# A Fourier filter and gated convolution on one core: the first input in longer rows over all DMA engines, the weights behind it, and the order laid out anew

## The chip, the cores and the metric

The kernel runs on one core of one Trainium2 chip. The metric is device time in microseconds (us) of one execution, the median of several runs. A profile is one further execution with the hardware profiler on; its times are counted from the first instruction.

## What is computed

Eight batches, each of 3200 positions by 256 channels, all float32 (three of the later weights come as float64). First a filter in frequency space:

```
X  = rfft(x, axis=1)
Yr = Xr @ w_r - Xi @ w_i + b_r
Yi = Xr @ w_i + Xi @ w_r + b_i
Y  = soft threshold of Yr and Yi at 0.01
y  = irfft(Y, n=3200)
```

Then a gated causal convolution of five taps on y:

```
gate = sigmoid(sum over k of conv_w[k] * y shifted by 4 - k)
out  = (gate * (y @ w_val)) @ w_out
```

## The kernel before

The transform of length 3200 is split as 64 x 50. For each batch the work goes through these steps, named by the tiles that appear in a profile:

- `x` is loaded in 8 blocks `u`, each of two halves `h`. A half is 50 rows of 4 KB; half 0 stands on partitions 0 to 49, half 1 on 64 to 113. TensorE (PE) multiplies it with `f1` (tile `f_sb`) into `p`, a copy keeps that as `s`, and a DMA stores it to `a_dram` in HBM. The store turns the two axes of the split.
- `a` is read back in 13 units of 128 rows. PE makes `s` (tile `s2`, printed `s`) from `a` and the matrix `f2`, then ScalarE (ACT) and VectorE (DVE) split it into a high and a low part (`xs`, `sx`), and PE does the complex product with the weights in `k_ps` (the sum of real and imaginary part) and `y_ps`. The weights `w_sb` are split likewise: `load_matrix` loads `w_r` and `w_i` into `st`, ACT casts the high part, DVE subtracts for the low part, and `sums` makes the sum and the difference of both.
- Bias and threshold follow (`yb`, `tp`), then `z_ps` (the first half of the way back), stored to `z_dram`, read back as `zl`, and `y_p`, which lands in `y_sb`. `turned` makes the way back's matrix `g1` from `f2` by PE with an identity, `eye`.
- The convolution runs on DVE (`acc`), `v_ps` and `o_ps` are the two products of the second layer.

What sets the order is `Plan`: every piece of work is entered by `add` with an engine, an estimated length, a place `at`, what it uses and what it sets. `Plan.order` plays the pieces through in time and takes on each engine, among those that could begin within `SLACK` of the first, the one with the smallest `at`. The table `O` shifts the `at` of each kind of work, `CLOCK`, `WIRE` and `BACKLOG` are its assumptions on PE and on transfers. What comes out is a fixed order of instructions on each engine; on the chip each engine follows its own, waiting for semaphores. Transfers are issued by SyncE (SP) and, at the start, by ACT. The compiled program gives the transfers eight semaphores in turn, so that an issue waits until the transfer eight places before it has landed.

The start of the program is written apart, in `p1_first`, for batch 0. It takes the eight blocks in four groups `v` of two. SP loads the halves `h = 0` and ACT the halves `h = 1`; each group gives 8 products on PE (16 instructions in a profile), a copy on DVE for one half and on ACT for the other, and four stores, two on SP and two on ACT. Two PSUM tiles of the kind `ps_2` hold a group's products, so the next group begins when both copies are done. Between the groups stand products `warm`, which compute nothing; `WARM` says how many. `STORED` stands for all stores of batch 0, and `load_f2` loads the matrix `f2` in four parts, the parts behind the first only after `STORED`. `load_bias` loads the two biases onto one partition, and PE spreads them over all partitions by six matmuls (lines 449 and 451). `from_float64` converts float64 weights to float32 in 13 steps on DVE, at `at + O["later"]`.

Of the kernel before, what the change touches and what calls it, by code (L numbers as in the profile page):

```python
# [32 lines left out]
def dft_constants():  # L33
# [46 lines left out]
class Plan:  # L80
# [30 lines left out]
    def order(self):  # L111
# [101 lines left out]
WEIGHTS = 130  # L213
CLOCK = ((40000, 1.6), (45000, 1.15))
WIRE = 230
BACKLOG = 5000


# [4 lines left out]
def act(n, kind="copy"):  # L223
# [5 lines left out]
T = float(NU)  # L229
O = {'hold': -1.089,  # L230
     'together': 2.272,
     'later': 4.406,
     'load_x': -3.369,
     'p1': 1.752,
     'p1_step': 1.14,
     'load_a': -3.927,
     's2': -1.558,
     's1i': 1.333,
     'p3': 3.595,
     'load_z': -3.135,  # L240
     'y': 0.522,
     'conv': 1.176,
     'val': 2.74,
     'gate': -3.751,
     'project': 5.91,
     'late_val': 7.079,
     'late_out': 15.503,
     'turn': 0.967,
     'mix_sum': -0.635,
     'p1_1': -0.586,  # L250
     'load_x_1': -0.349,
     'p1_2': -1.603,
     'p3_0': 0.549}
WARM = 2, 1, 1, 1, 10
SLOTS = {"x": 3, "zl": 3, "y_hl": 2, "s1": 2, "a": 3, "xs": 2, "sx": 2, "xz": 1, "yb": 2, "tp": 3, "zst": 2,
         "acc": 2, "g_hl": 2, "o": 2, "ps_s2": 2, "ps_y": 1, "ps_k": 1, "ps_2": 2, "a_dram": 2, "z_dram": 2}
# [6 lines left out]
def fourier_filter_then_gated_conv(ctx: ExitStack, tc: tile.TileContext, x, w_r, w_i, b_r, b_i,  # L263
# [57 lines left out]
    def load_matrix(at, name, w, dst):  # L321
# [87 lines left out]
    def load_f2(at, part):  # L409
        t = slice(PARTS[part] * 2 * P, min(PARTS[part + 1] * 2, NT) * P)  # L410
        add(at, "SP", 400, lambda: nc.sync.dma_start(out=f2_sb[:, t], in_=f2[:, t]), STORED if part else (), [("f2", part, 0)],
            kb=(t.stop - t.start) / 2)

# [14 lines left out]
    def load_bias(at):  # L428

        def load():  # L430
            for k, b in enumerate((b_r, b_i)):
                nc.sync.dma_start(out=b_sb[0:1, k * D:(k + 1) * D], in_=b.rearrange("(o d) -> o d", o=1))
        add(-91, "SP", 800, load, (), [("b", 0, 0)], kb=20)

        def marks():
# [3 lines left out]
            nc.gpsimd.memset(m[:, P + N1 + 1:], 1.0)  # L439
        add(-198, "POOL", 300, marks, (), [("b", 0, 1)])  # L440
        k2, k1 = ("bias_2", 0), ("bias_1", 0)
        m = lambda k: b_sb[0:1, 2 * D + k * P:2 * D + (k + 1) * P]

        def spread():
# [5 lines left out]
            for k in range(2):  # L450
                nc.tensor.matmul(q, m(k), b_sb[0:1, k * D:(k + 1) * D], start=k == 0, stop=k == 1)
        add(at, "PE", 2700, spread, [("b", 0, 0), ("b", 0, 1)], [k2 + (0,), k1 + (0,)], {k2: "ps_y", k1: "ps_k"}, mode="f")
        add(at + 0.01, "ACT", act(2 * D), lambda: nc.scalar.copy(out=bias_sb[:, 0:2], in_=tl[k2]), [k2 + (0,)], [("bias", 0, 0)])
# [30 lines left out]
    STORED = [("stored", 0, (u, h)) for u in range(8) for h in range(NH)]  # L484

    def p1_first(v, at):

        us = (2 * v, 2 * v + 1)
        src = x[0].rearrange("(n h m) c -> h n (m c)", h=NH, m=NM)
        engines = (("SP", nc.sync), ("ACT", nc.scalar))  # L490
        for u in us:
            kx, tag = ("x", (0, u)), "x" if u < 3 else "zl" if u < 6 else "y_hl"

            def load(h, u=u, kx=kx, tag=tag):
                xt = tl[kx] if h else room(kx, tag, 4 * D)
                engines[h][1].dma_start(out=xt[half(h), :], in_=src[h, :, u * 4 * D:(u + 1) * 4 * D])
            for h in range(NH):
                add(-100 + u, engines[h][0], 400, lambda h=h, load=load: load(h), (), [kx + (h,)], None if h else {kx: tag}, kb=200)
        kp = [("p1", (0, v, h)) for h in range(NH)]
# [3 lines left out]
        def products():  # L503
            p = [two_banks(kp[h]) for h in range(NH)]
            for j in range(2):
                for h in range(NH):
                    for k in range(2):
                        nc.tensor.matmul(p[h][k * HP:(k + 1) * HP, j, :], f1_sb[half(h), :],
                                         tl["x", (0, us[k])][half(h), j * 512:(j + 1) * 512], start=True, stop=True)

# [4 lines left out]
        def store(h, k):  # L515
            if ("a_dram", 0) not in tl:
                buffer(("a_dram", 0), "a_dram", [Q, NM * D])
            dst = tl["a_dram", 0].rearrange("(f h) mc -> h f mc", h=NH)
            engines[h][1].dma_start(out=dst[h, :, us[k] * 4 * D:(us[k] + 1) * 4 * D], in_=tl[ks[h]][k * HP:k * HP + N2, :])
        add(at, "PE", 1740, products, [("x", (0, u), h) for u in us for h in range(NH)] + [("f1", 0, 0)],  # L520
            [k + (0,) for k in kp] + [("turn", "p1", v)], {k: "ps_2" for k in kp}, mode="q")
        for h, eng in enumerate(("DVE", "ACT")):
            add(at + 0.01, eng, act(1024) if h else dve(1024), lambda h=h: keep(h), [kp[h] + (0,)],
                [ks[h] + (0,)] + ([START[h]] if v == 3 else []), {ks[h]: tag})
            for k in range(2):
                add(at + 0.02, engines[h][0], 400, lambda h=h, k=k: store(h, k), [ks[h] + (0,)], [("a_dram", 0, (us[k], h)), ("stored", 0, (us[k], h))],
                    {("a_dram", 0): "a_dram"} if (v, h, k) == (0, 0, 0) else None, kb=200)

    def p1(b, u, at):

        kx, kp, ks, ka = ("x", (b, u)), ("p1", (b, u)), ("s1", (b, u)), ("a_dram", b)
# [18 lines left out]
        def store():  # L550
# [4 lines left out]
            for k in range(2):  # L555
                lo = u * 4 * D + k * 512
                nc.sync.dma_start(out=dst[:, :, lo:lo + 512], in_=st[k * HP:k * HP + N2])
        add(at + O["load_x"] + O["load_x_1"] * (b == 1), "SP", 700, load, STORED if b == 1 else (), [kx + (0,)], {kx: "x"}, kb=400, chain="x")
        add(at, "PE", 890, products, [kx + (0,), ("f1", 0, 0)], [kp + (0,)], {kp: "ps_2"}, mode="q")
        add(at + 0.01, "ACT", act(1024), keep, [kp + (0,)], [ks + (0,)], {ks: "s1"})  # L560
        add(at + 0.02, "SP", 1500, store, [ks + (0,)], [ka + (u,)], {ka: "a_dram"} if u == 0 else None, kb=400)


# [421 lines left out]
```

## Time and profile before

| what | value |
| --- | --- |
| median of 3 runs | 900.66 us (899.45 to 905.88) |
| profiled execution, first to last instruction | 897.1 us |
| mean TensorE clock granted | 0.986 |
| PE busy | 865.2 us (96%) |
| weight loads (PEld) | 741.1 us (83%) |
| DVE busy | 763.5 us (85%) |
| ACT busy | 603.7 us (67%) |
| moved by DMA | 162.26 MB, mean 181 GB/s |

The profiled execution has no other time of its own than this span; the timed runs, which hold what lies around it too, take 3.6 us more in the median. In a profile, L508 is line 508 of the kernel; names of tiles stand as out<-in. PE is the matmul engine, PEld its weight loads, which run beside it; SPq and ACTq are the issues of transfers by SP and ACT. A matmul in float32 is counted as two instructions, so that `x8` can be four matmuls of the program. The share of DMA is the mean of the core's 16 DMA engines.

### The profile page before, as it was taken

Reading aid. Unit: us, or ns where it says so; the run is one execution under the profiler, and the core shown is the slowest. Engines: PE = TensorE matmul, PEld = TensorE weight load, DVE = VectorE, ACT = ScalarE, POOL = GpSimd, SP = SyncE. Lnnn points to the kernel's source line nnn. Section 1 sums busy time; section 2 is a strip of 40 time slices with the busy share of each in tenths; the row PEclk is TensorE's granted clock in tenths of the full one; section 3 lists DMA queues with packets and bytes.
Section 4 is the critical chain, followed back from the end, with each engine's and each line's share of the span. In section 5 each row is a group of like instructions: output and inputs, shape, how many; then the busy total and the mean of one; then the engine's idle time right before and its main releaser. Section 6 shows DMA issues by size and latency. Waiting matters only on the chain.

```text
span 897.1 us, 24381 instructions
## 1 busy us (share of the span) xinstructions
PE 865.2 (96%) x10370; PEld 741.1 (83%) x10370; DVE 763.5 (85%) x1139; ACT 603.7 (67%) x924; POOL 4.4 (0%) x11
## 2 busy tenths in 40 slices
PE   7799979999999999999999999999999999999898
PEld 2478758898888988899888988989788899998675
DVE  1267787999899997999789996999969998999896
ACT  1256656877677867777677876877757776875654
POOL 0000000000000000000000000000001000000000
PEclk8889999999999999999999999999999999999999
DMA  6577777635755476555674566645674453513522
GB/s 203 198 233 239 228 227 217 210 130 182 236 180 179 159 229 218 190 183 160 217 235 158 163 204 217 222 131 174 215 223 154 139 172 109 178 62 116 180 75 91
DMA packets 103439, 162.26 MB, mean 181 GB/s; under 512 B 9154, under 2 KB 77636, under 8 KB 103332
## 3 DMA queue, kind: packets, MB, share of 16 engines
q1 hardware_dynamic: 102372, 157.44, 54.8%
q10 hardware_dynamic: 960, 3.28, 1.1%
q8 instruction: 81, 1.33, 0.6%
q14 instruction: 26, 0.21, 0.1%
HBM read 82.04 MB, written 78.64 MB: 179 GB/s over the span
## 4 chain that ended last, share of the span: by engine, by line
PE 83%; DVE 10%; DMA 4%; ACT 2%; issue 1%; ACTq 1%; SPq 0%
PE y_ps L660 14%; PE o_ps L791 13%; PE v_ps L791 12%; PE s L590 10%; PE z_ps L703 9%; PE k_ps L665 8%; PE y_p L759 7%; PE p L543 6%; DVE acc L813 4%; DMA x<-in_x 1%; PE v_ps L787 1%; DVE acc L855 1%; DVE gated L317 1%; DMA f_sb<-in_f 1%; DMA a_dram<-s 1%
## 5 line engine op out<-in xcount | busy, mean ns | idle before, releaser
L813 DVE SCALAR_TENSOR_TENSOR acc<-y_sb,cw_sb,acc 128x800 f32<-128x800 f32 (+1 forms) x264 | 255.9, 1018 | 17.6 <-ACT acc L810 17.2
L660 PE MATMUL y_ps<-w_sb,xs 128*128 128x256 f32 x1152 | 155.4, 284 | 0.6 <-DVE xs L648 0.6
L791 PE MATMUL o_ps<-gated,wo_sb 128*128 128x400 f32 x756 | 155.2, 351 | 0.6 <-DVE acc L855 0.6
L660 PEld LDWEIGHTS y_ps<-w_sb,xs 128*128 128x128 f32 x1152 | 144.5, 189 | 11.3 <-DVE xs L652 3.2
L791 PEld LDWEIGHTS o_ps<-gated,wo_sb 128*128 128x128 f32 x756 | 133.5, 188 | 3.1 <-DVE acc L855 0.8
L791 PE MATMUL v_ps<-y_hl,wv_sb 128*128 128x400 f32 x660 | 131.3, 346 | 0.5 <-ACT o L879 0.5
L590 PE MATMUL s<-f_sb,a 128*128 128x128 f32 x800 | 113.2, 284 | 8.2 <-ACT wo_sb L315 3.4
L791 PEld LDWEIGHTS v_ps<-y_hl,wv_sb 128*128 128x128 f32 x660 | 118.5, 188 | 1.6 <-ACT o L879 0.9
L590 PEld LDWEIGHTS s<-f_sb,a 128*128 128x128 f32 x800 | 101.7, 196 | 20.8 <-issue 6.9
L678 ACT ACTIVATE tp<-yb,nlam 128x512 f32<-128x512 f32 (+1 forms) x104 | 73.7, 708 | 38.7 <-DVE yb L674 38.6
L665 PEld LDWEIGHTS k_ps<-w_sb,xs 128*128 128x128 f32 x576 | 77.2, 190 | 20.8 <-issue 10.5
L703 PE MATMUL z_ps<-tp,g_sb 64*64 64x256 f32 x1536 | 93.4, 381 | 0.0
L665 PE MATMUL k_ps<-w_sb,xs 128*128 128x256 f32 x576 | 91.1, 294 | 1.2 <-DVE yb L671 0.9
L759 PEld LDWEIGHTS y_p<-g_sb,zl 50*64 50x64 f32 x4096 | 68.3, 135 | 18.1 <-issue 7.3
L315 ACT CAST gated<-acc 128x800 fp32r<-128x800 f32 x63 | 54.3, 862 | 38.2 <-DVE acc L855 38.0
L759 PE MATMUL y_p<-g_sb,zl 50*64 50x50 f32 x4096 | 72.5, 219 | 7.1 <-issue 4.2
L680 DVE SCALAR_TENSOR_TENSOR tp<-yb,tp 128x512 f32<-128x512 f32 (+1 forms) x104 | 70.0, 673 | 10.6 <-ACT tp L678 10.5
L671 DVE TENSOR_TENSOR yb<-k_ps,bias_sb 128x512 f32<-128x512 f32 x96 | 65.6, 684 | 15.7 <-PE k_ps L665 15.6
L703 PEld LDWEIGHTS z_ps<-tp,g_sb 64*64 64x64 f32 x1536 | 55.3, 133 | 27.4 <-issue 5.1
L855 DVE TENSOR_TENSOR acc<-v_ps,acc 128x800 f32<-128x800 f32 x64 | 62.9, 984 | 16.1 <-PE v_ps L791 12.7
L674 DVE TENSOR_TENSOR yb<-y_ps,yb 128x512 f32<-128x512 f32 x96 | 65.5, 683 | 7.4 <-PE y_ps L660 6.9
L714 ACT COPY z_t<-z_ps 128x1024 f32<-128x1024 f32 x48 | 48.5, 1010 | 25.7 <-PE z_ps L703 25.1
(80 smaller groups left out, 1016.7 us busy)
## 6 DMA issues: line engine op xcount, KB each, us to landing
zl<-z_dram SPq DMA_DIRECT2D x128, 200.0 KB
out<-o SPq DMA_DIRECT2D x63, 400.0 KB
a<-a_dram SPq DMA_DIRECT2D x96, 256.0 KB
z_dram<-z_t SPq DMA_DIRECT2D x48, 512.0 KB
x<-in_x SPq DMA_DIRECT2D x120, 200.0 KB
a_dram<-s SPq DMA_DIRECT2D x120, 200.0 KB
x<-in_x ACTq DMA_DIRECT2D x8, 200.0 KB
a_dram<-s ACTq DMA_DIRECT2D x8, 200.0 KB
```

The costliest lines, as they stand in the source:

```text
L590: nc.tensor.matmul(spec()[:, c, :, i, :], tl[ka][:, i, c * P:(c + 1) * P], f2_of(i), start=True, stop=True)
L660: nc.tensor.matmul(p[:, 1 - r, :], xm(hx, c, r), w_sb[:, m, hw, c, :], start=k == 0, stop=k == 5)
L665: nc.tensor.matmul(p, sm(hx, c), w_sb[:, 0, hw, c, :], start=k == 0, stop=k == 5)
L671: nc.vector.tensor_tensor(out=buffer(kb, "yb", [P, 2, D]), in0=tl[kk].rearrange("p (a d) -> p a d", a=1).to_broadcast([P, 2, D]), in1=bias ...
L674: add(at + 0.2, "DVE", dve(2 * D), lambda: nc.vector.tensor_tensor(out=yb(), in0=tl[ky], in1=yb(), op=ALU.add), [ky + (0,)], [kb + (0,)])
L678: nc.scalar.activation(out=buffer(kt, "tp", [P, 2, D])[:, 0:n], in_=tl[kb][:, 0:n], func=AF.Relu, bias=nlam)
L680: add(at + 0.2, "DVE", dve(n * D), lambda: nc.vector.scalar_tensor_tensor(out=tl[kt][:, 0:n], in0=tl[kb][:, 0:n], scalar=LAM, in1=tl[kt][: ...
L703: nc.tensor.matmul(p[e * HP:(e + 1) * HP, i, j * D:(j + 1) * D], g[i * HP:(i + 1) * HP, r, e * HP:(e + 1) * HP], tl[kts[j]][i * HP:(i + 1) ...
L759: nc.tensor.matmul(pv[h][e * HP:(e + 1) * HP, c, m, :], zt[half(h), m, c * P + e * HP:c * P + (e + 1) * HP], g2_sb[half(h), :], start=True ...
L791: nc.tensor.matmul(p[:, e, 0:TB], w[:, hw, c, e * P:(e + 1) * P], src(hy, c), start=n == 0, stop=n == 5)
L813: nc.vector.scalar_tensor_tensor(out=acc(c), in0=y_of(c, j), scalar=cw_sb[:, c, j:j + 1], in1=acc(c), op0=ALU.mult, op1=ALU.add)
L855: add(at + O["gate"], "DVE", dve(2 * TB), lambda: nc.vector.tensor_tensor(out=gate(), in0=hn(tl[kv][:, :, 0:TB]), in1=gate(), op=ALU.mult) ...
```

## The change

Seven things are changed.

1. **First input.** `load_first` takes the place of the loads in `p1_first`. Blocks 0 to 6 go into the tile `y_sb` (the filtered signal, which is not written before the end of batch 0), seen as one wide tile, and block 7 into a buffer `x`. Each half is split into 48 and 2 rows (`ROWS`). The 48 rows move in rows of 8 KB for two blocks at a time; the 2 left over move once for blocks 0 to 6, with 28 KB in a row, and once for block 7.
2. **First stores**, and loads and stores of batch 1 in `p1`: split into 48 and 2 rows (96 and 4 in `p1`'s stores, which hold both halves).
3. **f1** is laid out for both halves by the host and comes in one transfer of 128 rows, issued by ACT.
4. **Biases.** One is loaded by SP, one by ACT, near the start, and PE spreads them ahead of the first group.
5. **Weights** `w_r`, `w_i`, the second part of `f2` and `eye` stand on SP behind the first stores (by the chain `rows`) and ahead of the first `a`.
6. **y_sb's zeros** (POOL) come behind the first products; `warm` writes into the tile `ps_s2`, and the first `WARM` is 1 instead of 2.
7. **The order**: other values in `O` (all but two), in `CLOCK`, three buffers `s1` instead of two.

```diff
-CLOCK = ((40000, 1.6), (45000, 1.15))
+CLOCK = ((22000, 1.4), (45000, 1.1))
-     'load_x': -3.369,
+     'load_x': 311.687,
-     'later': 4.406,
+     'later': 71.905,
...
-WARM = 2, 1, 1, 1, 10
+WARM = 1, 1, 1, 1, 10
-        add(at, "SP", 400, load, (), [key + (0,)], {key: "o"}, kb=256)
+        add(at, "SP", 400, load, (), [key + (0,)], {key: "o"}, kb=256, chain="rows")
...
+    ROWS = slice(0, 48), slice(48, N2)
+    wide = y_sb.rearrange("p c h n -> p (c h n)")
+    def first_x(u):
+        return wide[:, u * 4 * D:(u + 1) * 4 * D] if u < 7 else tl["x", (0, 7)]
+    def load_first():
+        src = x[0].rearrange("(n h m) c -> h n (m c)", h=NH, m=NM)
+        moves = (0, 2, 0), (0, 7, 1), (2, 4, 0), (4, 6, 0), (6, 7, 0), (7, 8, 0), (7, 8, 1)
+        for i, (u0, u1, tail) in enumerate(moves):
...
+                engines[h][1].dma_start(out=dst[half(h), :][r], in_=src[h, r, u0 * 4 * D:u1 * 4 * D])
...
-                engines[h][1].dma_start(out=xt[half(h), :], in_=src[h, :, u * 4 * D:(u + 1) * 4 * D])
...
-            engines[h][1].dma_start(out=dst[h, :, us[k] * 4 * D:(us[k] + 1) * 4 * D], in_=tl[ks[h]][k * HP:k * HP + N2, :])
+            for r in ROWS:
+                engines[h][1].dma_start(out=dst[h, r, us[k] * 4 * D:(us[k] + 1) * 4 * D], in_=tl[ks[h]][k * HP:k * HP + N2, :][r])
...
     def p1(b, u, at):
+        rows = ROWS if b == 1 else (slice(0, N2),)
...
-    load_matrix(-90, "w_r", w_r, w_sb[:, 0])
-    load_matrix(-89, "w_i", w_i, w_sb[:, 1])
-    sums(-88.9)
-    add(-88.5, "SP", 400, load_eye, (), [("eye", 0, 0)], kb=64)
-    load_f2(-88, 0)
-    load_bias(-30)
-    load_f2(-1.95, 1)
+    load_matrix(-27.9, "w_r", w_r, w_sb[:, 0])
+    load_matrix(-27.8, "w_i", w_i, w_sb[:, 1])
+    sums(-27.7)
+    load_f2(-27.7, 1)
+    add(-27.6, "SP", 400, load_eye, (), [("eye", 0, 0)], kb=64, chain="rows")
+    load_f2(-31, 0)
+    load_bias(-41)
```

How the order moves is seen at three places. The first is SP behind the first stores: `s_198` and `s_200` are the last group's copies, `st<-in_w_r` and `st<-in_w_i` the weights, `f_sb<-in_f 128x768` the second part of f2. Before:

```order
L519 DMA a_dram<-s_198 50x1024 x2
L574 DMA a<-a_dram 128x2x256 x2
L537 DMA x<-in_x 50x1024 x2
L411 DMA f_sb<-in_f 128x768
L574 DMA a<-a_dram 128x2x256
L537 DMA x<-in_x 50x1024 x4
```

And now:

```order
L535 DMA a_dram<-s_200 48x1024
L535 DMA a_dram<-s_200 2x1024
L329 DMA st<-in_w_r 128x2x256
L329 DMA st<-in_w_i 128x2x256
L413 DMA f_sb<-in_f 128x768
L914 DMA eye_sb<-in_eye 128x128
L593 DMA a<-a_dram 128x2x256 x3
L555 DMA x<-in_x 48x1024 x2
L555 DMA x<-in_x 2x1024 x2
```

Weights and identity, which stood ahead of the first stores, have moved behind them, and f2's second part from behind the loads of batch 1's `x` to ahead of the first `a`.

The second place is PE between the first products' last group and the first `k_ps`; `bias` is the spreading of the biases, `s_` with a number a unit's product with f2, `p_` with a number a block of batch 1. Before:

```order
L508 MATMUL p_180<-x,f_sb 64x512 x2
L424 MATMUL turned<-eye_sb,f_sb 128x128 x2
L907 MATMUL warm<-idle 128x512 x10
L590 MATMUL s_240<-f_sb,a 128x2x64 x2
L449 MATMUL bias_243<-b_sb 128x256 x4
L451 MATMUL bias_244<-b_sb 128x256 x2
L590 MATMUL s_240<-f_sb,a 128x2x64 x2
L590 MATMUL s_257<-f_sb,a 128x2x64 x4
L543 MATMUL p_270<-x,f_sb 64x512 x4
L543 MATMUL p_284<-x,f_sb 64x512 x4
L665 MATMUL k_ps<-w_sb,xs 128x256 x6
```

And now:

```order
L923 MATMUL warm<-idle 128x512 x10
L426 MATMUL turned<-eye_sb,f_sb 128x128 x2
L609 MATMUL s_264<-f_sb,a 128x2x64 x4
L426 MATMUL turned<-eye_sb,f_sb 128x128 x2
L609 MATMUL s_278<-f_sb,a 128x2x64 x4
L426 MATMUL turned<-eye_sb,f_sb 128x128 x2
L609 MATMUL s_297<-f_sb,a 128x2x64 x4
L684 MATMUL k_ps<-w_sb,xs 128x256 x6
L561 MATMUL p_319<-x,f_sb 64x512 x4
L684 MATMUL k_ps<-w_sb,xs 128x256 x6
```

The biases are gone from here (they stand ahead of the first group now), two more `turned` and one more `s` stand ahead of the first `k_ps`, and batch 1's products come behind it.

The third place is DVE where `w_out` is converted from float64 (`st_1256`, `st_1326` and `st_1327` are the conversion's buffers), in the passage from batch 0 to batch 1. Before:

```order
L647 TENSOR_TENSOR sx<-s_1217,sx 128x256
L356 TENSOR_SCALAR st_1256<-st_1110 128x512
L356 TENSOR_SCALAR st_1256<-st_1256 128x512 x3
L356 TENSOR_SCALAR st_1257<-st_1110 128x512
L362 TENSOR_TENSOR st_1257<-st_1257,st_1256 128x512
L356 TENSOR_SCALAR st_1256<-st_1110 128x512
L356 TENSOR_SCALAR st_1256<-st_1256 128x512
L362 TENSOR_TENSOR st_1256<-st_1256,st_1257 128x512
```

And now:

```order
L358 TENSOR_SCALAR st_1326<-st_1326 128x512 x3
L690 TENSOR_TENSOR yb<-k_ps,bias_sb 128x512
L358 TENSOR_SCALAR st_1327<-st_1136 128x512
L364 TENSOR_TENSOR st_1327<-st_1327,st_1326 128x512
L693 TENSOR_TENSOR yb<-y_ps,yb 128x512
L667 TENSOR_TENSOR xs<-s_1288,xs 128x512
L671 TENSOR_TENSOR xs<-sx,xs 128x256
L699 SCALAR_TENSOR_TENSOR tp<-yb,tp 128x512
L666 TENSOR_TENSOR sx<-s_1359,sx 128x256
L358 TENSOR_SCALAR st_1326<-st_1136 128x512
```

The conversion's thirteen steps stood in one piece, behind the `sx` of one unit (the first eight of them are seen here); now the filter's own steps stand between them.

More of the change, by code (lines that the diff above doesn't have):

```diff
@@ L410, in load_f2 @@
         t = slice(PARTS[part] * 2 * P, min(PARTS[part + 1] * 2, NT) * P)
-        add(at, "SP", 400, lambda: nc.sync.dma_start(out=f2_sb[:, t], in_=f2[:, t]), STORED if part else (), [("f2", part, 0)],
-            kb=(t.stop - t.start) / 2)
+        add(at, "SP", 400, lambda: nc.sync.dma_start(out=f2_sb[:, t], in_=f2[:, t]), STORED if part > 1 else (), [("f2", part, 0)],
+            kb=(t.stop - t.start) / 2, chain="rows" if part == 1 else None)
     def make_g1(at, u):
@@ L428, in load_bias @@
     def load_bias(at):
[L430 to L433, printed above, removed]
+        for k, (b, (name, eng)) in enumerate(zip((b_r, b_i), engines)):
+            add(-99.5, name, 400, lambda k=k, b=b, eng=eng: eng.dma_start(out=b_sb[0:1, k * D:(k + 1) * D], in_=b.rearrange("(o d) -> o d", o=1)), (),
+                [("b", 0, k)], delay=2600)
         def marks():
@@ L525, in p1_first @@
             for k in range(2):
-                add(at + 0.02, engines[h][0], 400, lambda h=h, k=k: store(h, k), [ks[h] + (0,)], [("a_dram", 0, (us[k], h)), ("stored", 0, (us[k], h))],
-                    {("a_dram", 0): "a_dram"} if (v, h, k) == (0, 0, 0) else None, kb=200)
+                add(at + 0.02, engines[h][0], 800, lambda h=h, k=k: store(h, k), [ks[h] + (0,)], [("a_dram", 0, (us[k], h)), ("stored", 0, (us[k], h))],
+                    {("a_dram", 0): "a_dram"} if (v, h, k) == (0, 0, 0) else None, kb=165, chain=None if h else "rows")
     def p1(b, u, at):
         kx, kp, ks, ka = ("x", (b, u)), ("p1", (b, u)), ("s1", (b, u)), ("a_dram", b)
+        rows = ROWS if b == 1 else (slice(0, N2),)
         def load():
@@ L535, in load @@
             src = x[b].rearrange("(n h m) c -> h n (m c)", h=NH, m=NM)
-            for h in range(NH):
-                nc.sync.dma_start(out=xt[half(h), :], in_=src[h, :, u * 4 * D:(u + 1) * 4 * D])
+            for r in rows:
+                for h in range(NH):
+                    nc.sync.dma_start(out=xt[half(h), :][r], in_=src[h, r, u * 4 * D:(u + 1) * 4 * D])
         def products():
@@ L556, in store @@
                 lo = u * 4 * D + k * 512
-                nc.sync.dma_start(out=dst[:, :, lo:lo + 512], in_=st[k * HP:k * HP + N2])
-        add(at + O["load_x"] + O["load_x_1"] * (b == 1), "SP", 700, load, STORED if b == 1 else (), [kx + (0,)], {kx: "x"}, kb=400, chain="x")
+                for r in rows:
+                    nc.sync.dma_start(out=dst[r, :, lo:lo + 512], in_=st[k * HP:k * HP + N2][r])
+        add(at + O["load_x"] + O["load_x_1"] * (b == 1), "SP", 700 * len(rows), load, STORED if b == 1 else (), [kx + (0,)], {kx: "x"}, kb=330 if b == 1 else 400, chain="x")
         add(at, "PE", 890, products, [kx + (0,), ("f1", 0, 0)], [kp + (0,)], {kp: "ps_2"}, mode="q")
         add(at + 0.01, "ACT", act(1024), keep, [kp + (0,)], [ks + (0,)], {ks: "s1"})
-        add(at + 0.02, "SP", 1500, store, [ks + (0,)], [ka + (u,)], {ka: "a_dram"} if u == 0 else None, kb=400)
+        add(at + 0.02, "SP", 2300 if b == 1 else 1500, store, [ks + (0,)], [ka + (u,)], {ka: "a_dram"} if u == 0 else None, kb=330 if b == 1 else 400)
     def p2(b, u, at):
@@ L891, in late_weights @@
         add(at, "POOL", 3000, make, [("a_dram", B - 1, 7), *[("w", n, h) for n in ("w_val", "w_out") for h in ("high", "low")]], [key + (0,)], {key: "x"})
-    def begin():
-        for h in range(NH):
-            nc.sync.dma_start(out=f1_sb[h * HP:h * HP + N2, :], in_=f1)
     def load_eye():
         nc.sync.dma_start(out=eye_sb, in_=eye)
-    add(-200, "SP", 800, begin, (), [("f1", 0, 0)], kb=20)
+    add(-200, "ACT", 400, lambda: nc.scalar.dma_start(out=f1_sb, in_=f1), (), [("f1", 0, 0)], delay=2800)
     ki, kw = ("idle", 0), ("warm", 0)
```

84 lines of the change are left out of this document (44 added, 40 removed).

## The prediction, made before the changed kernel was run

> **What bounds the kernel now.** I read the page first, then busy time by stretch, then the chain of work at the start.
>
> ```profile
> span 897.1 us, 24381 instructions
> ...
> 0.00:46.00 46.00, 34.88 (x119) 14.34 (x120) 9.88 (x13) 9.71 (x14) 1.14 (x9) 0.85 0.62 200
> 46.00:897.10 851.10, 830.29 (x10252) 726.79 (x10252) 753.64 (x1127) 593.97 (x910) 3.28 (x2) 0.99 0.56 180
> ```
>
> The first line is the page's. In the table of stretches the columns are length, busy time of PE, PEld, DVE, ACT, POOL, then PE's clock, DMA share and GB/s. Behind 46 us PE is busy 830.3 of 851.1 us: that part is bound by PE, and the change takes no product out of it. Before 46 us PE's 34.9 us hold the first products and many `warm` ones, which compute nothing. So what can be won is the start, and some of the 20.8 us of idle time behind it.
>
> How the start runs is told by PE's timeline and the chain (start, duration, what, and in brackets what ended an idle time):
>
> ```profile
> 8.75 3.78 PE L508 MATMUL p<-x,f_sb 50*64 50x512 f32 x14 [0.65 <-DMA x<-in_x]
> 14.47 2.35 PE L508 MATMUL p<-x,f_sb 50*64 50x512 f32 x16
> 18.28 2.04 PE L508 MATMUL p<-x,f_sb 50*64 50x512 f32 x16 [0.40 <-ACT s L513]
> 24.51 2.89 PE L508 MATMUL p<-x,f_sb 50*64 50x512 f32 x16 [3.13 <-ACT s L513]
> 39.42 0.71 PE L590 MATMUL s<-f_sb,a 128*128 128x128 f32 x4 [1.99 <-DMA a<-a_dram]
> ...
> 18.36 5.05 ACTq L519 DMA_DIRECT2D a_dram<-s  x4
> 23.45 1.01 ACT L513 COPY s<-p 128x1024 f32<-128x1024 f32 x1 [5.22 <-DMA a_dram<-s]
> 27.44 1.01 ACT L513 COPY s<-p 128x1024 f32<-128x1024 f32 x1 [2.98 <-PE p L508]
> ...
> 29.74 6.81 DMA a_dram<-s
> ...
> 38.41 7.31 DMA f_sb<-in_f
> ...
> 45.85 2.05 PE s L590 x8
> 47.90 2.67 PE p L543 x16
> 50.57 0.90 PE k_ps L665 x6
> ```
>
> Three delays follow each other. The fourth group of first products starts at 24.51, late, because ACT stood 5.05 us in the issue of stores before it could copy the third (23.45). The last stores land at 36.55 (29.74 + 6.81), 8.1 us after the last copy ended (27.44 + 1.01). And the second part of f2, issued at 38.41 behind loads of x, lands at 45.7, while the first `a` was there at 39.42. I follow all this to one mark, the first `k_ps`, at 50.57.
>
> **The change, part by part.** The engines' rates come first:
>
> ```profile
> 5.00:10.00 5.00, 2.53 (x11) 0.93 (x13) 0.00 (x0) 1.28 (x1) 0.00 (x0) 0.85 0.64 201
> 20.00:25.00 5.00, 1.87 (x11) 0.61 (x11) 1.22 (x1) 1.01 (x1) 0.00 (x0) 1.00 0.63 222
> ```
>
> With only 50-row transfers under way the DMA share stands at 0.63 to 0.64, ten of the sixteen engines: 201 GB/s / 10.2 = 19.6 GB/s for an engine when x is read, 222 / 10.1 = 22 when `a_dram` is written. 48 rows are three for each of sixteen engines where 50 were five for each of ten. The two rows left over go alone. Spread evenly they would make 3.1 rows on an engine, always on the same ones 4. I take 4, since the row shows that such transfers stay on their ten engines.
>
> [...] The share of 0.63 agrees with the ten; no row names an engine. [...]
>
> *First products.* Group 0 needs its 8 KB rows and the left-over rows of seven blocks: on the fullest engine 6 x 8 + 2 x 28 = 104 KB, 5.3 us at 19.6, and about 2 us for issue and landing (the `a` issued at 36.64 below was used 2.8 us later, 0.8 of it data), from 1.3 on: 8.6, as in the row at 8.75. Ahead of it PE now spreads the biases (1.99 + 1.16 us), hidden in that wait. ACT comes to its first copy behind nine issues, the table load (1.28) and two bias copies (0.58, the second half as large); the last issue waits for the blocks 2 and 3, 152 KB into the fullest engine, 7.8 us, so about 9.4. That gives 11.7, while group 0 ends at 12.5. So **groups 0 to 2 stay where they are**, however fast x comes: PE, copy and a `warm` set their pace, and the reads save nothing there.
>
> ```profile
> 36.64 0.91 SPq L574 DMA_DIRECT2D a<-a_dram  x2
> ...
> 8.41 1.28 ACT L513 ACT_TABLE_LOAD   x1 [8.41 <-DMA x<-in_x]
> ...
> 40.06 1.99 PE L449 MATMUL bias<-b_sb 1*128 1x256 f32 x8
> 41.89 1.16 PE L451 MATMUL bias<-b_sb 1*128 1x256 f32 x4
> 42.08 0.58 ACT L453 COPY bias_sb<-bias 128x512 f32<-128x512 f32 x1 [10.93 <-PE bias L449]
> 44.23 0.37 ACT L640 COPY sx<-s 128x256 f32<-128x256 f32 x1 [0.78 <-PE s L590]
> 50.69 0.41 ACT L651 CAST xs<-sx 128x256 fp32r<-128x256 f32 x1
> ...
> 28.42 1.28 DVE L341 SCALAR_TENSOR_TENSOR st<-st 128x512 f32<-128x512 f32 x2
> 29.63 2.50 DVE L317 TENSOR_TENSOR w_sb<-st,w_sb 128x512 fp32r<-128x512 f32 x4
> ```
>
> *Group 3.* At the pace of the two groups before it (18.28 - 14.47 = 3.8 us) it starts at 22.1 instead of 24.5: a group's stores are now 64 KB on the fullest engine, 2.9 us at 22 GB/s, less than the pace, so ACT no longer stands. What is queued behind ACT's issues is the next copy; that wait comes back if stores take over 3.8 us. Products end at 24.1, the copy at 25.2.
>
> *Stores.* 2.9 us of data and 2.0 around it: all in `a_dram` at 30.1 instead of 36.5.
>
> *Weights, f2, identity.* They now stand on SP's queue between the last stores and the first `a`: 512 + 384 + 64 = 960 KB at 16 x 22 = 352 GB/s are 2.8 us. SP can issue them as the last stores land, from about 28; their data run from 29 to 31.8, those of the weights to 30.5, landed at 31.5. The first `a` (256 KB, 0.8) follows: 32.6, used at 33.6. That costs it 0.7 us against 30.1 + 2.8. The stall for f2 is gone, and what is late next are the weights: 31.5, then a cast (0.6 for 512 elements, where 256 took 0.41), DVE's 1.28 + 2.50, and, since DVE does these in order, `sx` (0.33), ACT's 0.41 and one more DVE step as large for the sum of real and imaginary part: 31.5 + 0.6 + 3.8 + 1.1 = 37.0. The path through `a` ends earlier (33.6 + 0.9 + 1.4 = 35.9). So `k_ps` starts at **37.0 instead of 50.57: 13.6 us**. The work done ahead of it is the same: one more `s` and two more `turned` (0.89 + 0.88) for two p (1.72).
>
> ```profile
> 62.41 0.86 PE p L543 x8
> ...
> 64.17 0.89 PE s L590 x8
> ...
> 66.46 0.44 PE turned L424 x4
> ...
> 100.45 0.33 DVE sx L647
> ```
>
> *Clock.* After its idle time PE ran at about half speed: the `s` at 45.85 took 2.05 us and the same at 64.17 0.89, two p took 2.67 and later 1.72. These 2.1 us were lost ahead of the mark. Now they may fall into the wait for the weights, and cost nothing, or wholly behind the mark, and cost 2.1 again; since the idle time ends just there I take **1.7 back**.
>
> *Conversion of float64 weights.* `later` goes from 4.4 to 71.9, so DVE does these steps between others instead of in one piece.
>
> ```profile
> 126.99 0.42 DVE sx L647
> 127.42 0.35 DVE st L356
> ...
> 133.41 0.70 DVE st L362
> ...
> PE s L590 <- ACT wo_sb L315: 3.4, 1, 3.4
> ...
> 100.00:200.00 100.00, 94.55 (x1267) 79.91 (x1266) 89.80 (x166) 68.69 (x111) 0.00 (x0) 0.98 0.64 204
> ```
>
> The piece for `w_out` held DVE from 127.4 to 134.1 and PE for 3.4 us; all idle time from 100 to 200 is 5.5. DVE's work stays, and at 90% of that stretch some of the wait returns elsewhere: I take **2.0**, between a loss of 2 and a gain of 5.5.
>
> *The rest of the order.* Every batch is laid out anew from other weights, with the same work. I cost it at nothing; it is bounded below by the idle time that is left (20.8 - 5.5 = 15.3) and above by the rivals. The second batch's split loads and stores (84 issues on SP up to the first batch's last `a`, before 50) are hidden under PE, which is busy without a gap where the stretch quoted below (60 to 80) lies. The zeroing of `y_sb` on POOL moves behind the first products, where nobody needs it for 100 us. One `warm` less at the start, another tile for them and a third buffer `s1` cost nothing: PE waits for x there in any case.
>
> **Sum.** 13.6 - 1.7 + 2.0 = 13.9; a span of 897.1 - 13.9 = 883.2. The median of the timed runs, 900.66, lies 3.6 above the profiled span; carried over, that is 887.
>
> **Rivals.**
>
> *The wires give no more.* If sixteen engines move together no more than ten do (222 GB/s), stores still land 8.1 us after the last copy (+3.2) and the 960 KB take 4.3 us (+1.5): 892. For it: engines reading x run slower than those writing (19.6 to 22). Against it: in the stretch from 60 to 80, where transfers of 128 rows run among the others, more than ten engines are at work and more bytes move.
>
> ```profile
> 60.00:80.00 20.00, 20.00 (x205) 17.11 (x204) 13.35 (x24) 13.47 (x24) 0.00 (x0) 1.00 0.82 279
> ```
>
> That is 279 GB/s at a share of 0.82, 21 GB/s for an engine still.
>
> *Too many transfers: slower.* A queue issues only when an earlier transfer has landed; the build lets eight be open at once, and the left-over rows now take half of them.
>
> ```profile
> 1.37 3.97 DMA x<-in_x
> ...
> 89.73 0.40 SPq L574 DMA_DIRECT2D a<-a_dram  x1
> ...
> SPq L496 <- DMA x<-in_x: 5.5, 4, 2.2
> ```
>
> From issue to landing a transfer took 3.97 us (x) to 7.31 (f2). The place is SP in the first batch: 84 transfers by 3.97 / 8 are 42 us, under the 53 that this stretch of issues had (36.64 to 89.73); by 7.31 / 8 they are 77, 24 us too long: 887 + 24 = **911**. It decides from a mean of 5.0 us. Against it: a pair of rows is 8 KB and waits for little. [...]
>
> *The new order idles more.* PE idles 2.4% behind 46 us, and 5.5% in the stretch from 100 to 200. Halfway between, 4% of 851 us are 34, 13 more: 900, no change. What speaks for it is DVE, busy 753.6 of the 851.1 us, on which any order leans; against it, the two orders change products' kind about as often.
>
> *More than forecast.* No half clock behind the mark (1.7), all of the conversions' 5.5, and a few of the 15.3: 887 - 1.7 - 3.5 - 5 = 877.
>
> **How the numbers follow.** Forecast 0.60, more than forecast 0.09, wires 0.11, new order 0.13, transfers 0.07. The range reaches from 875 to 899 and leaves out most of the transfers, half of the new order and a little below. A measurement of this kernel tells about 1% (9 us) from no change: faster means below 891.7, slower above 909.7. Most of the forecast, all of the case above it and half of the wires lie below: 0.71; slower holds the transfers and the bad end of the order, 0.07; the rest, 0.22, is the same.
>
> **What would show it.** Right: a DMA share well over 0.63 in the first 30 us; the fourth group at 22; the last store landed by 30; no wait of an `s` for `f_sb`; the first `k_ps` at 37, released by the weights' split; no wait for `wo_sb`. Wrong: ACT still standing in its stores, a start of `k_ps` behind 42, or PE busy in less than 97% behind it.

## The result: 0.7% slower, and where the time went

The changed kernel takes 907.89 us in the median of 12 runs (903.42 to 912.38), the kernel before 901.17 beside it (898.52 to 910.12, 12 runs): a ratio of 1.007, with a 95% interval from 1.0042 to 1.0099. The forecast was 887 with a range from 875 to 899, so it was wrong. The profiled execution has a span of 904.4 us and a time of its own of 906.21, so 1.8 us lie around the span.

The page's first line, of the changed kernel:

```profile
span 904.4 us, 24476 instructions
```

Its busy time by stretches, columns as in the prediction:

```profile
0.00:46.00 46.00, 34.24 (x107) 14.33 (x108) 8.02 (x10) 8.05 (x11) 1.21 (x9) 0.99 0.82 180
46.00:904.40 858.40, 835.57 (x10263) 734.35 (x10262) 756.05 (x1130) 594.75 (x914) 3.85 (x2) 0.99 0.56 179
5.00:15.00 10.00, 5.23 (x12) 3.62 (x12) 0.00 (x0) 0.00 (x0) 0.00 (x0) 1.00 1.02 162
30.00:40.00 10.00, 9.90 (x37) 4.59 (x34) 2.45 (x2) 2.02 (x2) 0.00 (x0) 1.00 0.85 209
41.00:46.00 5.00, 2.18 (x7) 1.01 (x6) 2.63 (x5) 1.96 (x4) 0.00 (x0) 0.92 0.96 301
```

The DMA share did rise, as forecast: 0.82 over the start, 1.02 while x is read, which is all sixteen engines. But the last column fell. While x is read the sixteen engines move 162 GB/s (166 in the stretch from 5 to 10), where ten moved 201 before. That is 10.4 GB/s for an engine instead of 19.6: all are busy, but their packets take longer. Between 41 and 46 us, where the weights' transfers of 128 rows run, 301 GB/s pass.

The timeline of its start (start, duration, what):

```profile
2.23 9.88 ACTq L504 DMA_DIRECT2D y_sb<-in_x  x4
11.81 2.07 PE L450 MATMUL bias<-b_sb 1*128 1x256 f32 x4 [3.99 <-DMA b_sb<-in_b_i]
15.52 4.32 PE L523 MATMUL p<-y_sb,f_sb 50*64 50x512 f32 x16
22.98 3.79 PE L523 MATMUL p<-y_sb,f_sb 50*64 50x512 f32 x16 [1.14 <-ACT s L528]
28.45 1.95 PE L523 MATMUL p<-y_sb,f_sb 50*64 50x512 f32 x16
31.55 0.64 PE L523 MATMUL p<-y_sb,f_sb 50*64 50x512 f32 x1
```

And its chain, in the same columns:

```profile
5.97 13.58 DMA y_sb<-in_x
19.86 1.28 ACT L454
21.89 1.04 ACT s L528
31.53 3.82 DMA a_dram<-s
41.12 4.14 DMA eye_sb<-in_eye
51.47 0.71 PE k_ps L684 x6
```

Group 0 starts at 15.52 instead of 8.75. PE first waits 3.99 us for the second bias, which had been issued at 1.67. By the packets' records its 1 KB started only at 9.43, as a 28 KB packet of SP's left-over rows ended (9.39). The 48 rows of blocks 0 and 1 had all ended at 7.28, but the left-over rows on ACT's queue, which group 0 needs too, ended at 14.44. ACT cannot copy before 19.86: it stands in its own issues of x until 19.82, and the chain counts 13.58 us of that as a wait for x. So every group is late, the fourth at 31.55 instead of 24.51. The first `k_ps` comes at 51.47 instead of 50.57.

Behind the first `k_ps` some 6.6 us more are lost. I split that stretch for PE into idle time, the loss to half clock (half the length of the stretches in which the trace records half clock, from the mark to PE's last instruction) and the rest. The mark here is the timeline's, 0.1 to 0.2 ahead of the chain's.

| kernel | first `k_ps` | from there to the end | PE idle | lost to half clock | busy without that loss |
| --- | --- | --- | --- | --- | --- |
| before | 50.5 | 846.6 | 16.6 | 3.4 | 822.4 |
| changed | 51.2 | 853.2 | 18.9 | 10.2 | 820.1 |

(About 4 us at the end, when PE is done, are in both.) Idle time rose by 2.3 and the loss to half clock by 6.8; the rest fell by 2.3, which I did not trace. So most of it is half clock. PE's longest waits behind 60 us, of the changed kernel (columns: sum, number, longest):

```profile
PE y_p L778 <- DMA zl<-z_dram: 3.7, 3, 2.7
PE p L561 <- DMA x<-in_x: 2.7, 1, 2.7
PE k_ps L684 <- DVE xs L671: 2.4, 1, 2.4
PE z_ps L714 <- DVE acc L874: 2.1, 1, 2.1
```

The wait for x ends at 71.4 us, those for `xs` and the longest for `zl` at 141.0 and 151.0. Stretches around them:

```profile
72.00:80.00 8.00, 8.00 (x58) 7.01 (x54) 3.92 (x8) 4.36 (x10) 0.00 (x0) 0.79 0.88 212
100.00:200.00 100.00, 93.94 (x1282) 79.04 (x1282) 86.17 (x163) 65.31 (x108) 0.00 (x0) 0.95 0.59 191
140.00:160.00 20.00, 15.88 (x162) 12.12 (x162) 13.28 (x27) 10.03 (x16) 0.00 (x0) 0.74 0.37 122
```

Two of the same stretches before:

```profile
72.00:80.00 8.00, 8.00 (x88) 7.10 (x81) 5.47 (x10) 5.30 (x10) 0.00 (x0) 1.00 0.79 267
140.00:160.00 20.00, 20.00 (x417) 16.74 (x410) 16.25 (x26) 14.93 (x23) 0.00 (x0) 1.00 0.71 225
```

Around and behind these waits the clock stood at 0.79 and 0.74, where before it was 1.00. The three waits are 7.8 us, and the records of half clock behind them, 13.7 us long, cost 6.8 more: here a wait of 2 to 3 us nearly doubles. It is not always so. The version with ten engines and 8 KB rows below waited 2.1 us at 63.8 and 2.4 at 132.4, and no half clock followed either at once.

### The profile page after: what moved, and what is told of

Read it like the earlier page. It is cut to its first block, busy times and chain, and to the rows that moved or that the text cites. A ratio compares the mean times of both kernels' runs of the same rounds, so it can differ in the third digit from the quotient of the medians.

```text
span 904.4 us, 24476 instructions
## 1 busy us (share of the span) xinstructions
PE 869.8 (96%) x10368; PEld 748.7 (83%) x10368; DVE 764.1 (84%) x1139; ACT 602.8 (67%) x924; POOL 5.1 (1%) x11
## 4 chain that ended last, share of the span: by engine, by line
PE 82%; DVE 8%; DMA 5%; ACT 2%; issue 1%; SPq 1%; ACTq 0%
PE y_ps L679 15%; PE o_ps L810 13%; PE v_ps L810 13%; PE s L609 10%; PE z_ps L722 8%; PE k_ps L684 7%; PE y_p L778 7%; PE p L561 6%; DVE acc L832 3%; DMA y_sb<-in_x 2%; DMA a_dram<-s 1%; DMA zl<-z_dram 1%; DVE acc L874 1%; PE v_ps L806 1%; DVE yb L693 1%
## 5 line engine op out<-in xcount | busy, mean ns | idle before, releaser
L832 DVE SCALAR_TENSOR_TENSOR acc<-y_sb,cw_sb,acc 128x800 f32<-128x800 f32 (+1 forms) x264 | 263.6, 1025 | 11.8 <-ACT acc L829 11.0
L679 PE MATMUL y_ps<-w_sb,xs 128*128 128x256 f32 x1152 | 159.7, 289 | 0.0
L810 PE MATMUL o_ps<-gated,wo_sb 128*128 128x400 f32 x756 | 157.5, 356 | 0.0
L810 PEld LDWEIGHTS o_ps<-gated,wo_sb 128*128 128x128 f32 x756 | 136.4, 191 | 3.4 <-ACT tp L697 0.4
L684 PE MATMUL k_ps<-w_sb,xs 128*128 128x256 f32 x576 | 88.4, 289 | 2.5 <-DVE xs L671 2.4
L663 ACT CAST xs<-s 128x512 fp32r<-128x512 f32 x96 | 56.2, 586 | 45.7 <-PE y_ps L679 38.4
L693 DVE TENSOR_TENSOR yb<-y_ps,yb 128x512 f32<-128x512 f32 x96 | 66.0, 688 | 24.0 <-PE y_ps L679 23.8
L778 PE MATMUL y_p<-g_sb,zl 50*64 50x50 f32 x4096 | 74.8, 223 | 10.4 <-issue 5.8
L874 DVE TENSOR_TENSOR acc<-v_ps,acc 128x800 f32<-128x800 f32 x64 | 63.2, 988 | 11.9 <-PE v_ps L810 5.5
```

The costliest lines, as they stand in the source:

```text
L679: nc.tensor.matmul(p[:, 1 - r, :], xm(hx, c, r), w_sb[:, m, hw, c, :], start=k == 0, stop=k == 5)
L684: nc.tensor.matmul(p, sm(hx, c), w_sb[:, 0, hw, c, :], start=k == 0, stop=k == 5)
L693: add(at + 0.2, "DVE", dve(2 * D), lambda: nc.vector.tensor_tensor(out=yb(), in0=tl[ky], in1=yb(), op=ALU.add), [ky + (0,)], [kb + (0,)])
L778: nc.tensor.matmul(pv[h][e * HP:(e + 1) * HP, c, m, :], zt[half(h), m, c * P + e * HP:c * P + (e + 1) * HP], g2_sb[half(h), :], start=True ...
L810: nc.tensor.matmul(p[:, e, 0:TB], w[:, hw, c, e * P:(e + 1) * P], src(hy, c), start=n == 0, stop=n == 5)
L832: nc.vector.scalar_tensor_tensor(out=acc(c), in0=y_of(c, j), scalar=cw_sb[:, c, j:j + 1], in1=acc(c), op0=ALU.mult, op1=ALU.add)
```

## The experiments

The timed runs of the kernel before spread from 894 to 912 us over all of this, so single executions (the first six) are not told apart by their time, but by the marks and rates in their traces. The theories were, at first: the distance of 64 KB between the rows read, the length of 8 KB rows, and sixteen engines crowding each other; later also the left-over rows.

**Shorter rows, sixteen engines.**

```diff
-                engines[h][1].dma_start(out=dst[half(h), :][r], in_=src[h, r, u0 * 4 * D:u1 * 4 * D])
+                for v in range(u0, u1) if not tail else ():
+                    o = 0 if u0 == 7 else (v - u0) * 4 * D
+                    engines[h][1].dma_start(out=dst[half(h), o:o + 4 * D][r], in_=src[h, r, v * 4 * D:(v + 1) * 4 * D])
...
```

> The changed kernel with the 48 rows of the first input in rows of 4 KB, one block at a time, the two left-over rows as they are; order and all else the same. Length theory (8 KB rows are what is slow): packets of 4 KB near 160 to 200 ns, x at over 250 GB/s, all x landed by 15 us, first k_ps at about 46. Crowding theory (sixteen engines that read rows 64 KB apart get no more than ten, and disturb each other): x still at 150 to 190 GB/s, landed at 18 to 20 us, first k_ps at 50 to 52.

**Ten engines, 50 rows of 8 KB, no left-over rows** (`dst[half(h), :]` from `src[h, :, ...]`, two blocks at a time).

> The changed kernel with the first input in 50 rows of 8 KB, nothing left over, so ten engines; order the same. Length theory: slow as in the changed kernel, 150 to 170 GB/s, x landed at 19. Crowding theory: 200 to 230 GB/s as with 50 rows before, x landed at 16, first product group at 9 or 10 instead of 15.5.

**Ten engines, 50 rows of 4 KB** (the same with one block at a time).

> The changed kernel with the first input in 50 rows of 4 KB as before the change, into the new place and in the new order. Both theories: 200 to 230 GB/s, x landed at 16 to 17, and what is then left against the kernel before is the order alone: first k_ps at 47 to 49.

**Sixteen engines, rows of adjacent memory.** Batch 0's x is read from other positions, so that the rows of a transfer lie side by side in HBM.

> The changed kernel reading the same number of bytes, in rows of 8 KB and 48 plus 2, but from rows that follow each other in memory (8 KB apart instead of 64 KB), so it transforms the wrong positions of batch 0. Pitch theory (rows 64 KB apart are what is slow): over 300 GB/s, 8 KB packets at 320 to 400 ns, x landed by 12 us, first k_ps at 43 to 45. Crowding or length theory without the pitch: 150 to 190 GB/s still.

Measured, in this order: 904.56, 899.38, 900.75 and 906.75 us beside 900.82 for the kernel before; first `k_ps` at 50.1, 46.4, 43.9 and 53.4. The stretch from 5 to 15 us, first with shorter rows:

```profile
5.00:15.00 10.00, 6.96 (x20) 4.18 (x24) 0.00 (x0) 0.00 (x0) 0.00 (x0) 1.00 0.90 176
```

With ten engines and 8 KB:

```profile
5.00:15.00 10.00, 7.71 (x24) 4.40 (x28) 0.00 (x0) 2.24 (x3) 0.00 (x0) 1.00 0.65 216
```

With ten engines and 4 KB:

```profile
5.00:15.00 10.00, 8.68 (x28) 4.44 (x28) 0.00 (x0) 1.98 (x3) 0.00 (x0) 1.00 0.66 225
```

With adjacent memory:

```profile
5.00:15.00 10.00, 5.64 (x12) 3.65 (x12) 0.00 (x0) 0.00 (x0) 0.00 (x0) 1.00 1.02 157
```

Adjacent memory does not help (157): the distance of the rows falls as a theory. Their length matters little (162 to 176). Ten engines move more than sixteen (216, 225), but without the left-over rows. The packets say that these are a part of it at most: in the changed kernel, between 2 and 20 us, an 8 KB packet took 826 ns in the mean while a 28 KB one was in flight, and still 660 at other times, where it took about 410 with ten engines. That left crowding, but crowding at what? The packets' records gave the hint. Packets in flight on SP's and on ACT's queue of the changed kernel, each 0.25 us from 3 us on:

```
15/0 14/0 11/2 8/6 6/9 3/11 2/14 0/15 0/16 0/18 0/16 2/14 6/10 9/7 10/6 13/3 15/2 15/1 17/0 16/0
```

The two queues are served by turns: in 13 of these 20 samples one of them has two packets in flight or fewer. SP's queue writes partitions 0 to 47, ACT's 64 to 111, so at most of these moments nearly all packets in flight write one half of the partitions. The next two runs keep the sixteen engines, and between them only the rows of a transfer differ, and with them the partitions that it writes. If writing one half at a time is what limits, every second partition should go faster than a block. Both read other positions of x, 1.28 times the bytes, without left-over rows.

**64 partitions in a block, or every second one.** Both queues read 64 rows at a time, each half of the columns. The twin against the block:

```diff
-                    to = slice(g * HP, (g + 1) * HP)
+                    to = slice(g, P, 2)
                     engines[h][1].dma_start(out=dst[to, lo + h * n:lo + (h + 1) * n], in_=rows[to, u0 * 4 * D + h * n:u0 * 4 * D + (h + 1) * n])
```

> The changed kernel with its first read of x replaced: both queues move 64-row pieces at once, each half of the columns; first all of partitions 0 to 63, then all of 64 to 127, row after row of adjacent memory (other positions of x, 1.28 times the bytes, no left-over rows; the output is of that data). [...] Theory of too many large packets in flight: sixteen engines are slow whatever the partitions, about 165 GB/s in this kernel and in its twin with every second row alike. Theory of the left-over pieces (they alone held the sixteen engines back): 300 GB/s and more in both.

> The twin of the run with blocks of 64 partitions: the same bytes, row size, queues and number of transfers, but each transfer writes every second partition, so that both halves of the partitions are written all the time. [...] Too many large packets: as the blocks, about 165 GB/s. Left-over theory: as the blocks, 300 GB/s.

The stretch while x is read, of the block:

```profile
4.00:14.00 10.00, 6.88 (x20) 4.38 (x24) 0.00 (x0) 0.00 (x0) 0.00 (x0) 1.00 1.04 221
```

Of its twin:

```profile
4.00:10.00 6.00, 4.66 (x11) 3.74 (x12) 0.00 (x0) 0.00 (x0) 0.00 (x0) 1.00 0.99 374
```

The same bytes, queues and engines move at 221 GB/s into a block and at 374 into every second partition; a 4 KB packet takes about 310 ns in the one and 159 in the other. The first `k_ps` follows, 50.7 and 44.6, with 906.97 and 901.89 us for the single executions. (The rows read lie 32 KB apart in the one and 64 in the other; the run with adjacent memory speaks against that as the cause.) So which partitions are written sets the rate here, 221 against 374 GB/s on sixteen engines, and crowding as such is refuted. That it is the half of the partitions that is crowded fits these two runs; for 48 rows it is argued. By what mechanism, no run here shows.

**Whole rows everywhere, and the old order.** The first of these two undoes the split into 48 and 2 rows also for the stores and for batch 1, with PE's order unchanged; the second takes the old `O` and `CLOCK` as well.

```diff
...
-        rows = ROWS if b == 1 else (slice(0, N2),)
+        rows = (slice(0, N2),)
...
```

> The changed kernel with whole 50-row transfers everywhere: the first read in 4 KB rows of 50 (as in the run e3_ten4, which gave the first k_ps at 43.9 us and 855.0 us from there to the end), and also the stores of the first four groups and the second batch's reads and stores, which the change had split into 48 and 2 rows. TensorE's order is that of e3_ten4. If the split of stores and of the second batch is what the rest loses, the stretch behind the first k_ps falls from 855 towards 847 and the time to about 892; if the split cost nothing there, the time stays at 900.8 within 0.3 per cent; if sixteen engines help the stores, the first k_ps comes later than 43.9.

> As the whole-row version, with the kernel before's numbers for the order and for its model of the clock; the other parts of the change (one buffer for the first read, biases spread first, weights and inverse factors behind the rows, third buffer of the first products' results) stay. If the new order is what is lost behind the first k_ps, that stretch falls from 855 to about 847 or, without the wait for the output weights and f2, to 844, and the time is 889 to 893; if the order costs nothing, as the prediction had it, the time is that of the whole-row version within 0.3 per cent.

Measured: 896.47, a ratio of 0.9958 (0.9912 to 1.0005), and 898.52, 0.9992 (0.9960 to 1.0024). Neither reached the gain that was expected if the splits or the order were what is lost (892, and 889 to 893). The traces, with those that follow:

| kernel | first `k_ps` | from there to the end | PE idle | lost to half clock | busy without that loss |
| --- | --- | --- | --- | --- | --- |
| whole rows | 45.5 | 852.9 | 17.3 | 11.9 | 819.6 |
| whole rows, old order | 47.6 | 850.1 | 18.8 | 5.1 | 822.1 |
| 96 + 4 rows | 46.7 | 895.0 | 37.6 | 23.9 | 829.4 |
| 96 + 4, old order | 49.0 | 846.6 | 14.1 | 7.6 | 820.9 |
| the same, no `warm` between | 47.2 | 845.0 | 13.3 | 7.5 | 820.2 |

The splits cost the start 51.2 - 45.5 = 5.7 us in all. The parts differ in sign: with only the first read whole (the ten engines and 4 KB above) `k_ps` came at 43.9, and with the stores whole too at 45.5. The fourth group starts at 23.8 and 23.7 in these two, but the last packet of the stores ends at 34.1 with 48 rows and at 35.5 with 50. So the split helped the stores and hurt the read. With batch 1 whole, the wait for x near 70 us is gone. The stretch from 60 to 70 of the changed kernel:

```profile
60.00:70.00 10.00, 8.74 (x88) 6.71 (x86) 7.29 (x14) 5.42 (x9) 0.00 (x0) 1.00 0.65 174
```

And with whole rows:

```profile
60.00:70.00 10.00, 10.00 (x101) 8.08 (x104) 6.82 (x13) 6.76 (x14) 0.00 (x0) 1.00 0.85 268
```

The order: the old numbers take 2.8 us off the stretch behind the mark (6.8 less half clock) and give 2.1 back ahead of it. Just behind the mark they wait 2.3 us for an `a`, with 1.7 lost to half clock after it, which still belongs to the start. In time the two versions cannot be told apart, their intervals overlap.

**Rows across both halves.** If writing one half at a time is the limit (221 GB/s in the block), every transfer should cross both halves. In these versions, built on the one with whole rows, row n of half h stands on partition 2n + h, the matrix `f1` is spread over both parities, and a block of x takes one product over 100 partitions. Even blocks are loaded and stored by SP, odd ones by ACT: in the first version 100 rows at a time, on ten engines, in the other two 96 and 4.

```diff
...
+        src = x[0].rearrange("(q m) c -> q (m c)", m=NM)
...
+                    engines[u % 2][1].dma_start(out=first_x(u)[r], in_=src[r, u * 4 * D:(u + 1) * 4 * D])
...
+                    nc.tensor.matmul(p[:, j, :], f1_sb[0:Q, HP:], first_x(u)[0:Q, j * 512:(j + 1) * 512], start=True, stop=True)
...
```

> [...] If the partitions do not matter: 205 to 220 GB/s and 45 us as in e7. The products cost TensorE 3.4 us a pair of blocks instead of 2.0, which matters only if the groups and not the rows set the pace.

> As the 100-row version, with each load and store in 96 rows on sixteen engines and 4 rows behind them on four. TensorE's order is the same. [...] Sixteen engines too many, whatever the partitions: no faster than the 100-row version, 165 GB/s, first k_ps at 47 or later.

> As the 96-row version, with the kernel before's numbers for the order and its model of the clock. By the account of the stretch behind the first k_ps (the new order's waits of over 2 us are each followed by 3.4 to 6.8 us of half clock, 10.8 us lost against 5.0 before), that stretch should lose 4 to 7 us at half clock rather than 10 to 13 and be 2 to 4 us shorter than in the 96-row version; the time 886 to 890. If the order costs nothing: as the 96-row version within 0.3 per cent.

Measured: 947.85 (1.0524, 1.0475 to 1.0573), 944.56 (1.0498, 1.0450 to 1.0546) and 896.66 (0.9961, 0.9936 to 0.9985). The first two lie some 45 us above the kernel before, though their starts are better than the changed kernel's (`k_ps` at 48.3 and 46.7): behind the mark they need 899.4 and 895.0. Against the whole-row version only the pieces of the start had changed, yet the planner, with the changed kernel's numbers, laid out all eight batches differently, with twice the idle time. With the old numbers the same start needs 846.6 there; the third version still missed the 886 to 890 expected of it. So a table `O` that gave 853 us behind one start can give 895 behind another.

Sixteen engines on 96 rows moved 229 GB/s, more than the 165 that would have spoken for too many engines. Ten engines on 100 rows moved 229 in the same stretch, so with both halves crossed the six more engines gained nothing. Why 96 rows stay so far below the 374 of every second partition, no run here shows. The stretch from 4 to 14 us of the third version:

```profile
4.00:14.00 10.00, 8.28 (x16) 5.16 (x17) 0.00 (x0) 0.13 (x1) 0.00 (x0) 1.00 0.99 229
```

And its timeline of PE; at 3.6 us for two blocks, and 0.86 for the `warm` behind them, PE now set the pace of the groups:

```profile
11.10 8.03 PE L518 MATMUL p<-y_sb,f_sb 100*128 100x512 f32 x12
18.97 1.02 PE L912 MATMUL warm<-idle 128*128 128x512 f32 x2
19.84 3.60 PE L518 MATMUL p<-y_sb,f_sb 100*128 100x512 f32 x8
23.27 1.02 PE L912 MATMUL warm<-idle 128*128 128x512 f32 x2
24.13 3.60 PE L518 MATMUL p<-y_sb,f_sb 100*128 100x512 f32 x8
```

**No idle products between them.**

```diff
-            lambda v=v: warm(WARM[v]),
+            lambda v=v: warm((1, 0, 0, 0, 11)[v]),
```

> As the 96-row version in the kernel before's order (e11), without the three idle products of 0.86 us between the pairs of first products (one more behind them); all other instructions stand where they stood. In e11 the pairs began at 11.1, 19.8, 24.1 and 28.4 us, 4.3 us apart, of which 3.6 is products. If TensorE sets the pace there, they are 3.5 us apart, the last begins near 26 and the first k_ps comes at 46 to 47 instead of 49.0, about 894 us; if the rows or the stores set it (a wait of TensorE between the pairs, or stores that land no earlier), the first k_ps stays at 49 and the time at 896 to 897; if the idle products kept the clock up, there is half clock among the pairs and the time is 898 or more.

Measured: 893.18 us (888.94 to 897.21, 12 runs), a ratio of 0.9914 (0.9883 to 0.9946). It is faster than both kernels. As expected PE ran through its first products without half clock (1.00 from 11 to 28 us), and the first `k_ps` came at 47.2. The timeline of PE:

```profile
11.47 15.45 PE L518 MATMUL p<-y_sb,f_sb 100*128 100x512 f32 x28
26.76 1.88 PE L518 MATMUL p<-x,f_sb 100*128 100x512 f32 x4
28.48 9.61 PE L912 MATMUL warm<-idle 128*128 128x512 f32 x22
37.92 1.95 PE L598 MATMUL s<-f_sb,a 128*128 128x128 f32 x16
```

And the end of the chain:

```profile
36.80 7.35 DMA x<-in_x
47.31 1.58 PE k_ps L673 x6
```

That is what is left: the old order puts two of batch 1's products ahead of the first `k_ps`, and they wait for their x. An order made for this start was not tried.

## Why the prediction was wrong, step by step

The forecast span was 883.2 us, the measured one 904.4. Of these 21.2 us about 11.7 arise until the first stores are in `a_dram` (30.1 forecast; the last packet ended at 41.62 and the first `a` was issued at 41.87), 2.7 from there to the first `k_ps`, and 6.9 behind it.

- **The rate, the step that failed first.** "19.6 GB/s for an engine", taken from ten engines, was carried over to sixteen. Measured were 166 / 16 = 10.4. The rows of before showed the engines' share, and I read the share as the limit; nothing in them said whether sixteen engines would keep that rate. The rival "the wires give no more" had the right sign, but stopped at 222 GB/s: that sixteen engines could move less than ten was in none of the cases, and so the range ended too early.
- **"Groups 0 to 2 stay where they are"**: refuted. It rested on x and the second bias landing by 8.6; group 0 began at 15.52 and group 2 at 28.45. The 104 KB that were put on the fullest engine would take some 10 us at 10.4 GB/s where 5.3 were counted. The four rows on it, that is, left-over rows always on the same engines, no run shows, since no trace names an engine; what the trace shows are four packets of 28 KB for blocks 0 to 6, about 2.9 us each, the last of them ended at 14.44. I also had ACT through its issues at about 9.4. It was 19.82, since an issue waits for the transfer eight places before it, and that moved at half the rate.
- **Group 3 at 22.1**: 31.55. Its own mechanism failed too: ACT still stood in its stores (three waits, 9.1 us in all). Stores on sixteen engines moved 209 GB/s where I took 352.
- **Weights, f2 and identity behind the rows**: right in kind, too large in size. From the first `a`'s issue (41.87) to `k_ps` it took 9.6 us instead of 13.9, and the wait for f2 is gone; forecast were 6.9, from 30.1 to 37.0. Last in the chain was `eye` (landed at 45.26), not the weights' split. Behind it PE had three `turned` and three `s` to do, 6.1 us, the first `turned` and `s` at half clock. The prediction's path through `a` counted one `s` of 0.9 there and 1.4 for the split.

```profile
45.40 1.20 PE turned L426 x4
46.60 1.71 PE s L609 x8
48.31 0.65 PE turned L426 x4
48.95 0.89 PE s L609 x8
49.85 0.45 PE turned L426 x4
50.31 1.16 PE s L609 x8
```

The whole-row version shows what these parts are worth without the split: `k_ps` at 45.5, 5.0 us earlier than before. Forecast were 13.6.

- **Half clock, 1.7 back**: wrong in place. A record of 3.4 us at half clock lies ahead of the mark, which costs 1.7 there, but behind it the loss rose from 3.4 to 10.2.
- **Conversion, a gain of 2.0**: the wait for `wo_sb` (3.4) went as forecast, but a wait of 2.4 for `xs` came, and one for `zl` (2.7) stands 10 us behind. DVE was not short of time there: it stood 3.07 us itself, in front of one of the conversion's steps, and `xs` came behind it.

```profile
138.21 0.43 DVE L358 TENSOR_SCALAR st<-st 128x512 int32<-128x512 int32 x1 [3.07 <-PE y_p L778]
```

`from_float64` has its buffers from the kind `zl`, which `y_p` reads, so the step could begin when a `y_p` was done; spread between other work, the conversion holds up what follows it on DVE. PE was busy 93.94 us of the stretch from 100 to 200 instead of 94.55, a loss of 0.6. But the half clock recorded there grew from 3.4 to 10.2 us, which is 3.4 more lost: by that estimate 4.0 in all, beyond the bound of a loss of 2.

- **"The rest of the order. I cost it at nothing"**: behind the mark idle time rose by 2.3 and the loss to half clock by 6.8, of the 6.6 us that are more there (the rest fell by 2.3). The bound of 15.3 counted idle time alone and left out half clock, which the trace records behind four of the waits. The rival "the new order idles more" had this, at 13 us.
- **"Too many transfers"**: one wait of 2.7 us for batch 1's x, gone with whole rows, not 24 us.

What stays open: the left-over rows were not run apart from the 48. Their 28 KB packets took about 2.9 us each, the second bias and group 0 stood behind them, so a part of the 5.7 us may be theirs. That sixteen engines on 48 rows move less than ten on 50 because of the partitions they write is argued from the twins with 64 rows; 96 rows across both halves gained nothing over 100 on ten engines. That waits cause the half clock is argued from their sequence in the trace; no run took a single wait away, and not every wait has half clock behind it. The marks and stretches come from one execution of each version.

## What to carry to other kernels

Before spreading a transfer over more engines, ask which partitions those engines write at one moment: here a busy share near 1 came with a lower rate, and the same bytes moved at 221 or 374 GB/s by the partitions alone. Read a share together with the rate, and do not carry a rate for one engine over to more of them: 19.6 GB/s on ten became 10.4 on sixteen. Look at the clock behind a wait of TensorE when you price it. When a start is rebuilt, look at the order of the rest again: the same table of numbers gave 853 and 895 us behind two starts.

## What the runs showed of the hardware

- Sixteen DMA engines moved 162 GB/s into partitions 0 to 47 and 64 to 111 by turns, 221 into blocks of 64, 229 and 242 into 96 consecutive partitions and 374 into every second partition; ten engines moved 201 to 225 into 50 partitions of each half, and 229 into 100.
- Two queues that write the two halves did not keep both filled: in 13 of the 20 samples above one of the queues had two packets in flight or fewer.
- Four waits of TensorE of 2.1 to 2.7 us in the changed kernel were followed by 3.4 to 6.8 us at half clock; two of 2.1 and 2.4 us in the version with ten engines and 8 KB rows were not.
